# A change to weight loads, the transposes of h, row sums and unread products in a fused attention and expert kernel

## The chip, the cores and the metric

The kernel runs on one core of a Trainium2 chip. The metric is the device time of one execution in microseconds. The other cores of the chip do nothing for it. All inputs and outputs lie in the chip's main memory as 32-bit floats; inside the core the kernel works in 16-bit floats, and its loads convert on the way.

## What is computed

Sliding-window attention over 8 batches of 8 heads, 576 positions and 64 columns per head, followed by a soft mixture of experts over the 4608 rows of 512 columns that the attention gives. There are 8 experts with 4 slots each.

```python
def _attn_ref(q, k, v):                       # q, k, v: [8, 8, 576, 64]
    scores = 1.0 / np.sqrt(D) * np.matmul(q, k.transpose(0, 1, 3, 2))
    mask = (rel >= 0) & (rel < 64)            # rel = row minus column
    attn = softmax(np.where(mask, scores, -1e9))
    return np.matmul(attn, v)

def _moe_ref(x, phi, w1, w2):                 # x [4608, 512], phi [512, 32], w1 [8, 512, 1024], w2 [8, 1024, 512]
    logits = x @ phi
    d = softmax of logits over the rows (axis 0)
    slot_input = (d.T @ x).reshape(8, 4, 512)
    for e in range(8):
        slot_out[e] = np.maximum(slot_input[e] @ w1[e], 0.0) @ w2[e]
    c = softmax of logits over the 32 slots (axis 1)
    return c @ slot_out                       # [4608, 512]
```

q, k and v are 28.3 MB together, w1 and w2 16.8 MB each, and the output is 9.4 MB.

## The kernel before

**Two parts.** The first part goes through 16 units; a unit is half of the heads of one batch (`units`, line 58). Each unit has three steps j. In a step the tensor engine (PE) transposes v (`stage_t2`), multiplies k with q (`stage_s`), transposes pieces of the next batch's q, k and v (`stage_t1`) and multiplies the exponentials with v (`stage_av`). After both halves of a batch, `stage_xt`, `stage_logit`, `stage_ex` and `stage_slot` (taken from the list `todo`, one per step) transpose the batch's rows, form exp(logits) in `ET` and add to the slot inputs in `acc`. The last batch has its own version (`fin_...`, lines 547 to 567). From unit 2 on (`MAN = 14`, line 508) the order on PE, the scalar engine (ACT) and the vector engine (DVE) is the order of the program.

The second part starts when the slot inputs are complete. For each expert e: `expert_h(e)` multiplies the slot inputs with w1 (h is 4 slots by 1024, kept as four groups of 256 columns), `expert_t(e)` transposes h by products with `sel`, a view of the identity, and `expert_o(e, half)` multiplies with w2 into `sop[half]`. `row_sums(bp)` (line 621) adds up the columns of `ET` for a pair of batches, so that `crcp` holds the reciprocals for the second softmax; it is called for experts 0 to 3 (line 674). `stir(8)` (line 613) is eight products whose result nobody reads; it stands ahead of `expert_o(7, 0)`. Then `slots_out(half)` moves the result into `slot_oa`, and `combine` multiplies `ET` with it, scales by `crcp` and sends pieces of the output off through SP's queue. The first six pieces are done in column halves (`early`), the others whole (`late`).

**Loads.** Nearly all loads are issued by POOL in program order, on one queue: per batch q, k, v in rows of 4608 bytes (`load_batch`, line 67), and between them the weights in the order of `w_order` (line 481), a few per batch (`issue_loads`, line 485). A weight of one expert is 2 MB at its source. `load_w(e, n)` (line 83) loads w1 in two pieces (n = 0, 1) of 1 MB with 8-KB rows, and w2 in two pieces (n = 2, 3): for experts 0 to 5 with 4-KB rows, for the last two (`NLAST`) by columns with 1-KB rows. The order of the last loads is w1 of experts 6 and 7, then the first column half of w2 of both, then the second halves. `w2_of` says where the rows of a product with w2 lie. Since w2's rows are dealt to partitions in twos, `expert_t` takes every second column of h (`f::2`) in two products of 128 columns.

POOL's DMAs use eight semaphores in turn: a DMA waits until the one eight places before it has landed. Tiles come from pools that are used in turn too, so that a load also waits for the last reader of the tile it replaces: two buffers each for `qn`, `kn`, `vn`, and the two halves of w2 of experts 4 to 6 take such buffers (`w2h`).

Of the kernel before, what the change touches and what calls it, by code (L numbers as in the profile page):

```python
# [16 lines left out]
def kernel(  # L17
# [10 lines left out]
    nc = tc.nc  # L28
# [45 lines left out]
    w1_t, w2_t = {}, {}  # L74
    NLAST = 2

    def w2_of(e, f, cols):

        if e >= E - NLAST:
            return w2_t[e, cols.start // (D // 2)][:, f, :]  # L80
        return w2_t[e, f // 4][:, f % 4, cols]

    def load_w(e, n):
# [4 lines left out]
        if n == 2 and (e < E - 4 or e == E - 1):  # L88
            if e < E - 4:
                t = pw2.tile([128, NFC, D], FP16, name="w2s", tag="w2s")  # L90
            else:
                t = pxb.tile([128, NFC, D], FP16, name="w2l", tag="x_bp")
            for m in range(2):
# [6 lines left out]
        if n < 2:  # L100
            c = slice(2 * n, 2 * n + 2)
            nc.gpsimd.dma_start(out=w1_t[e][:, c], in_=moe_w1[e].rearrange("(p c) f -> p c f", p=128)[:, c])  # L102
        elif cols:
            c = slice(D // 2 * (n - 2), D // 2 * (n - 1))
            nc.gpsimd.dma_start(out=w2_t[e, n - 2], in_=moe_w2[e].rearrange("(c p) d -> p c d", p=128)[:, :, c])
        else:
            g = slice(2 * n - 4, 2 * n - 2)
            nc.gpsimd.dma_start(out=w2_t[e, n - 2].rearrange("p (g c) d -> p g (c d)", c=2),
                                in_=moe_w2[e].rearrange("(g p c) d -> p g (c d)", p=128, c=2)[:, g])
# [224 lines left out]
    def stage_xt(b, part):  # L334
# [11 lines left out]
        if part < 2:  # L346
            nc.vector.tensor_copy(out=moe[b][:, :, 2 * part:2 * part + 2, :],
                                  in_=tr[:, :, :].rearrange("p (k n) q -> p k n q", n=2))
# [129 lines left out]

    w_order = [(e, n) for e in range(E - NLAST) for n in range(4)]
    last = range(E - NLAST, E)
    w_order += [(e, n) for e in last for n in range(2)] + [(e, n) for n in range(2, 4) for e in last]

    def issue_loads(u):
        if u == 1 or u > 1 and u % 2 == 0:
            b = u // 2 + 2
            if b < B:
                load_batch(b)
                for _ in range(2 + b % 2):  # L490
                    load_w(*w_order.pop(0))
            else:

                for _ in range(len(w_order) if u > nu - 4 else 8):
                    load_w(*w_order.pop(0))

    load_batch(1)
    load_w(*w_order.pop(0))
    todo = []
# [10 lines left out]
    for u in range(nu):  # L510
# [7 lines left out]
        for j in range(3):  # L518
# [15 lines left out]
            if pend is not None:  # L534
# [5 lines left out]
                if pj == 2 and units[pu][1] == 1:  # L540
                    b = units[pu][0]
                    todo += [lambda b=b, p=p: stage_xt(b, p) for p in range(2 + b % 2)]
                    todo += [lambda b=b: stage_logit(b), lambda b=b: stage_ex(b), lambda b=b: stage_slot(b)]
            pend = (u, j)
# [43 lines left out]
    def expert_t(e):  # L588

        th = ps2.tile([128, 2, 4, SPE], FP32, name="th", tag="cp", bufs=4)  # L590
        for f in range(2):
            c = h_t[e][:, f::2] if e < E - NLAST else h_t[e][:, 128 * f:128 * f + 128]
            nc.tensor.matmul(th[:, f], c, sel[:, :, SPE * e:SPE * e + SPE], start=True, stop=True)
        hT = hTs[e % NLAST]
        if e >= NLAST:
            nc.vector.memset(hT[:, :, SPE * (e - NLAST):SPE * (e - NLAST) + SPE], 0.0)
        nc.vector.tensor_copy(
            out=hT[:, :, SPE * e:SPE * e + SPE].rearrange("p (g f) s -> p f g s", f=2), in_=th[:, :])
# [14 lines left out]
    def stir(n):  # L613

        if "stir" not in h_t:
            h_t["stir"] = ps2.tile([128, 256], FP32, name="stir", tag="hp")
        for _ in range(n):
            nc.tensor.matmul(h_t["stir"][:, :], ident[:, :], ET[:, 0, 0:256], start=True, stop=True)


    def row_sums(bp):
        rs = ps2.tile([128, T], FP32, name="rs", tag="cp", bufs=4)
        for j in range(T):
            nc.tensor.matmul(rs[:, j:j + 1], ET[:, bp, j::T], quarter[:, :], start=True, stop=True)
        nc.vector.reciprocal(crcp[:, bp, :], rs[:, :])
# [27 lines left out]
    with tc.manual_schedule(engines={mybir.EngineType.PE, mybir.EngineType.Activation, mybir.EngineType.DVE}):  # L653
# [10 lines left out]
        for e in range(E):  # L664
# [4 lines left out]
            if e > E - NLAST:  # L669
                stir(8)  # L670
# [3 lines left out]
            if e < B // 2:  # L674
                row_sums(e)
        slots_out(0)
        for n, p in enumerate(early):
            combine(*p, halves[0])
            if n >= len(early) - NLAST:
# [36 lines left out]
```

The softmax here doesn't subtract the row's maximum and nothing guards it: scores larger than these inputs give would overflow.

## Time and profile before

| What | us |
|---|---|
| median of 7 runs (179.59 to 180.77) | 180.36 |
| profiled execution, its own time | 180.72 |
| span of the profiled execution | 178.9 |
| PE busy | 138.2 (77%) |
| ACT busy | 121.5 (68%) |
| DVE busy | 117.8 (66%) |
| POOL busy | 40.1 (22%) |
| read from main memory | 61.93 MB |
| written to main memory | 9.44 MB |

The span is what the engines' instructions cover; some 1.8 us of the time lie around it. The DMA rate in the profile counts bytes at the destination: while loads convert 32 bits to 16, twice as many bytes leave the source. PE's clock is full until 148 us and half in some stretches after it. The attention part takes until about 133 us, the products of the experts until 150 us, and the output from 151 us to the end.

### The profile page before, as it was taken

How to read it: one execution, taken by the hardware profiler on the slowest of the kernel's cores; microseconds unless marked ns; L12 is line 12 of the kernel's file. 1: busy time of each engine (PE TensorE's matmuls, PEld its weight loads, DVE VectorE, ACT ScalarE, POOL GpSimd, SP SyncE). 2: the span in 40 equal slices, each digit the busy share in tenths (PEclk: the TensorE clock that was granted, in tenths of full speed). 3: DMA queues.
4: the chain of work that ended last, by engine and by line, in shares of the span. 5: the costliest groups of instructions: out<-in, count | busy, mean ns of one | idle time of the engine just before them, and what ended most of it. 6: DMA issues, size and time to landing. Idle time of an engine off the chain costs nothing.

```text
span 178.9 us, 6645 instructions
## 1 busy us (share of the span) xinstructions
PE 138.2 (77%) x2929; PEld 101.9 (57%) x2929; DVE 117.8 (66%) x283; ACT 121.5 (68%) x202; POOL 40.1 (22%) x65
## 2 busy tenths in 40 slices
PE   0659977997999997989989798888879976888200
PEld 0448766775777775767667576655556743444000
DVE  5634869769787888876876977597862212599300
ACT  2656696996998898789699598943644223699300
POOL 8601634212132133121232122222311000000000
PEclk9999999999999999999999999999999996699855
DMA  5999999999999999999999999999999999999994
GB/s 176 310 205 212 213 212 216 209 212 212 218 210 210 212 211 213 214 211 212 213 213 210 214 212 215 210 214 211 213 213 216 197 198 151 336 351 411 427 422 188
DMA packets 22812, 41.71 MB, mean 233 GB/s; under 512 B 1792, under 2 KB 10496, under 8 KB 22784
## 3 DMA queue, kind: packets, MB, share of 16 engines
q0 software_dynamic: 16784, 30.08, 90.7%
q1 hardware_dynamic: 6000, 11.21, 16.6%
q8 instruction: 23, 0.38, 0.8%
q14 instruction: 5, 0.04, 0.1%
HBM read 61.93 MB, written 9.44 MB: 399 GB/s over the span
## 4 chain that ended last, share of the span: by engine, by line
PE 38%; ACT 22%; DMA 16%; DVE 13%; issue 4%; SPq 1%; ACTq 0%
DMA w2l<-in_moe_w_dram 12%; PE tr L192 11%; ACT pm L281 6%; DVE vT L197 6%; ACT qT L199 6%; PE tr L236 5%; DMA first<-in_v_dram 4%; PE sc L264 4%; ACT ob L640 4%; PE cp L636 4%; PE av L307 3%; PE sc L271 3%; PE tr L345 3%; ACT kT L199 3%; DVE x_bp L315 3%
## 5 line engine op out<-in xcount | busy, mean ns | idle before, releaser
L281 ACT ACTIVATE pm<-sc 128x1024 f16<-128x1024 f32 (+1 forms) x46 | 38.1, 828 | 16.9 <-PE sc L271 16.9
L199 ACT COPY qT<-tr 128x640 f16<-128x640 f16 (+1 forms) x30 | 23.4, 865 | 1.4 <-PE tr L192 1.4
L199 ACT COPY kT<-tr 128x640 f16<-128x640 f16 (+1 forms) x30 | 23.7, 880 | 0.2 <-PE tr L192 0.2
L315 DVE TENSOR_TENSOR x_bp<-av,rc 128x512 f16<-128x512 f32 x32 | 22.1, 691 | 1.1
L307 PE MATMUL av<-vw,pm 128*64 128x65 f16 x576 | 19.3, 197 | 3.1 <-DVE x_bp L315 1.0
L197 DVE COPY vT<-tr 128x512 f16<-128x512 f16 (+1 forms) x17 | 13.9, 836 | 8.3 <-PE tr L192 8.3
L192 PE MATMUL tr<-ident,qn 128*64 128x128 f16 x288 | 13.6, 234 | 7.0 <-ACT qn L502 5.3
L271 PE MATMUL sc<-qT,kT 64*128 64x64 f16 x576 | 17.9, 193 | 1.2 <-DVE kT L197 0.9
L642 DVE TENSOR_SCALAR ob<-cp,crcp 128x256 f32<-128x256 f32 (+1 forms) x25 | 13.9, 588 | 7.5 <-PE cp L636 7.3
L271 PEld LDWEIGHTS <-kT 64*128 64x128 f16 x576 | 15.1, 97 | 5.7 <-ACT kT L199 1.1
L307 PEld LDWEIGHTS <-pm 128*64 128x64 f16 x576 | 15.7, 112 | 4.4 <-DVE x_bp L315 1.9
L264 PE MATMUL sc<-rep,hide 64*128 64x512 f16 (+1 forms) x96 | 17.1, 342 | 1.1 <-ACT pm L281 1.1
L640 ACT ACTIVATE ob<-cp,crcp 128x256 f32<-128x256 f32 (+1 forms) x26 | 13.9, 563 | 2.5 <-PE cp L636 1.8
L192 PEld LDWEIGHTS <-qn 128*64 128x64 f16 x288 | 10.1, 116 | 9.1 <-ACT qn L502 5.3
L192 PE MATMUL tr<-ident,vn 128*64 128x128 f16 x288 | 12.9, 232 | 2.9 <-ACT kT L199 1.1
L236 PE MATMUL tr<-ident,vT 128*128 128x128 f16 x128 | 10.5, 224 | 5.9 <-DVE rc L313 3.6
L199 ACT COPY vT<-tr 128x640 f16<-128x640 f16 x15 | 14.0, 933 | 1.4 <-PE tr L192 1.3
L636 PE MATMUL cp<-slot_oa,ET 128*128 128x256 f16 (+1 forms) x51 | 12.8, 351 | 2.7 <-ACT slot_oa L611 0.9
L102 POOL DMA_DIRECT2D w1s<-in_moe_w_dram x16 | 8.9, 554 | 21.1 <-DMA w1s<-in_moe_w_dram 7.3
L237 DVE COPY vw<-tr 128x1024 f16<-128x1024 f16 x16 | 11.0, 689 | 3.7 <-PE tr L236 3.7
L236 PEld LDWEIGHTS <-vT 128*128 128x128 f16 x128 | 8.1, 100 | 9.2 <-ACT vT L199 6.5
L192 PE MATMUL tr<-ident,kn 128*64 128x128 f16 x288 | 12.3, 233 | 0.1
(115 smaller groups left out, 228.7 us busy)
## 6 DMA issues: line engine op xcount, KB each, us to landing
w1s<-in_moe_w_dram POOLq DMA_DIRECT2D x16, 512.0 KB, 20.6
out_dram<-ob SPq DMA_DIRECT2D x6, 768.0 KB, 7.7
w2s<-in_moe_w_dram POOLq DMA_DIRECT2D x8, 512.0 KB, 20.4
qn<-in_q_dram POOLq DMA_DIRECT2D x7, 576.0 KB, 20.5
kn<-in_k_dram POOLq DMA_DIRECT2D x7, 576.0 KB, 20.8
vn<-in_v_dram POOLq DMA_DIRECT2D x7, 576.0 KB, 19.1
w2h<-in_moe_w_dram POOLq DMA_DIRECT2D x6, 512.0 KB, 20.2
out_dram<-ob SPq DMA_DIRECT2D x8, 384.0 KB, 4.3
```

The source lines that it names most:

```text
L192: nc.tensor.transpose(tr[64 * x:64 * x + 64, j, :], src[:, x, 64 * (t0 + j):64 * (t0 + j) + 64], ident[:, :])
L197: nc.vector.tensor_copy(out=o, in_=i)
L199: nc.scalar.copy(out=o, in_=i)
L236: nc.tensor.transpose(tr[:, 2 * w + h, :], vT[:, h, 64 + 128 * w:192 + 128 * w], ident[:, :])
L264: nc.tensor.matmul(sc[x][:, 0:128 * n], hide[64 * x:64 * x + 64, :], rep[64 * x:64 * x + 64, 0:2 * n, :], start=True, stop=False, skip_gro ...
L271: nc.tensor.matmul(sc[x][:, o:o + 64], st["kT"][64 * x:64 * x + 64, h, 64 * i:64 * i + 128], st["qT"][64 * x:64 * x + 64, h, 64 * i:64 * i ...
L281: nc.scalar.activation(pm[:, :, 0:2 * n, :], sct[:, :, 0:128 * n].rearrange("p x (w q) -> p x w q", q=64), AF.Exp, scale=scale)
L307: nc.tensor.matmul(av[r0:r0 + 64, kk, 65 * (w // 2):65 * (w // 2) + 65], pm[:, x, h * n + w, :], st["vw"][:, i, 2 * h + x, 0:65], start=Tr ...
L315: nc.vector.tensor_tensor(out=xb[:, c0:c0 + 2, 256 * half:256 * half + 256].rearrange("p c (k d) -> p k c d", d=64), in0=avv[:, :, :, 0:64 ...
L636: nc.tensor.matmul(cp[:, :], ET[:, bp, j::T], slot_oa[:, cols], start=True, stop=True)
L640: nc.scalar.activation(ob[:, g, :], cp[:, :], AF.Copy, scale=cr)
L642: nc.vector.tensor_scalar(out=ob[:, g, :], in0=cp[:, :], scalar1=cr, scalar2=None, op0=ALU.mult)
```

## The change

**w1** is loaded in one DMA of 2 MB with 16-KB rows, instead of two with 8-KB rows.

**w2 of experts 0 to 5** is dealt to partitions in fours, so that rows are 8 KB, in two DMAs of 1 MB. For expert 2 (`ES`) the load is cut another way: three lots of 4 partitions and a fourth one, each preceded by a small load of 2 or 12 partitions from phi (`pass_over`, into a tile nobody reads), and then the other 112 partitions in one DMA. That is nine DMAs of POOL's queue in place of two.

**Order of the loads.** The first weight load is now the first half of w2 of expert 0, then its w1. A w1 counts as two in the number of weight loads per batch, and the debt is carried over (`want`). The nine DMAs of expert 2 count as one.

**expert_t** for experts 0 to 5 makes h's transpose in eight products of 64 columns instead of two of 128. Those of experts 6 and 7 are as before.

**Row sums** of pairs 0, 1 and 2 are made in the three steps of unit 14, that of pair 3 ahead of `expert_o(6, 0)`. **Unread products**: one in each step of units 14 and 15 (five in all), and nine instead of eight ahead of `expert_o(7, 0)`.

**stage_xt** of batch 6 copies with ACT instead of DVE. **In the early pieces**, `expert_o(6, 1)`, `expert_o(7, 1)` and `slots_out(1)` come one piece earlier.

```diff
+    def w2_strips(e, p0, p1):
+        nc.gpsimd.dma_start(
+            out=w2_t[e][p0:p1].rearrange("p (g c) d -> p g (c d)", c=4),
+            in_=moe_w2[e].rearrange("(g p c) d -> p g (c d)", p=128, c=4)[p0:p1])
+    turns = []
+    def pass_over(n):
+        if not turns:
+            turns.append(const.tile([12, 4, 2, 16], FP16, name="turn"))
+        t = turns[0][0:n, len(turns) - 1]
+        turns.append(n)
+        nc.gpsimd.dma_start(out=t, in_=moe_phi[0:2 * n, 0:16].rearrange("(p c) s -> p c s", c=2))
...
-        if n < 2:
-            c = slice(2 * n, 2 * n + 2)
-            nc.gpsimd.dma_start(out=w1_t[e][:, c], in_=moe_w1[e].rearrange("(p c) f -> p c f", p=128)[:, c])
+        if n == 0:
+            nc.gpsimd.dma_start(out=w1_t[e].rearrange("p c f -> p (c f)"),
+                                in_=moe_w1[e].rearrange("(p c) f -> p (c f)", p=128))
...
-            g = slice(2 * n - 4, 2 * n - 2)
-            nc.gpsimd.dma_start(out=w2_t[e, n - 2].rearrange("p (g c) d -> p g (c d)", c=2),
-                                in_=moe_w2[e].rearrange("(g p c) d -> p g (c d)", p=128, c=2)[:, g])
+        elif e == ES:
+            if n == 2:
+                for i in range(4):
+                    pass_over(12 if i else 2)
+                    w2_strips(e, 4 * i, 4 * i + 4)
+                w2_strips(e, 16, 128)
+        else:
+            nc.gpsimd.dma_start(out=w2_t[e, n - 2].rearrange("p c d -> p (c d)"),
+                                in_=moe_w2[e].rearrange("(g p c) d -> g p (c d)", p=128, c=4)[n - 2])
...
+            o, i = moe[b][:, :, 2 * part:2 * part + 2, :], tr[:, :, :].rearrange("p (k n) q -> p k n q", n=2)
+            if b == B - 2:
+                nc.scalar.copy(out=o, in_=i)
+            else:
+                nc.vector.tensor_copy(out=o, in_=i)
...
-    w_order = [(e, n) for e in range(E - NLAST) for n in range(4)]
+    w_order = [(e, n) for e in range(E - NLAST) for n in (0, 2, 3)]
-    w_order += [(e, n) for e in last for n in range(2)] + [(e, n) for n in range(2, 4) for e in last]
+    w_order += [(e, 0) for e in last] + [(e, n) for n in range(2, 4) for e in last]
...
-                for _ in range(2 + b % 2):
-                    load_w(*w_order.pop(0))
+                want[0] += 2 + b % 2
+                while want[0] > 0:
+                    e, n = w_order.pop(0)
+                    load_w(e, n)
+                    want[0] -= 1 if n else 2
...
-                for _ in range(len(w_order) if u > nu - 4 else 8):
+                for _ in range(len(w_order) if u > nu - 4 else 5):
                     load_w(*w_order.pop(0))
...
+    w_order[0:2] = [(0, 2), (0, 0)]
     load_w(*w_order.pop(0))
+    want = [0]
...
+            if u == nu - 2:
+                row_sums(j, ps, "tr")
+            if u >= nu - 2:
+                stir(1, ps, "tr", 4)
...
-        for f in range(2):
-            c = h_t[e][:, f::2] if e < E - NLAST else h_t[e][:, 128 * f:128 * f + 128]
-            nc.tensor.matmul(th[:, f], c, sel[:, :, SPE * e:SPE * e + SPE], start=True, stop=True)
+        th = ps2.tile([128, 4, 2, SPE], FP32, name="th", tag="cp", bufs=4)
+        for c in range(4):
+            for x in range(2):
+                nc.tensor.matmul(th[64 * x:64 * x + 64, c], h_t[e][:, c::4], sel[:, x::2, slots], start=True, stop=True)
+        nc.vector.tensor_copy(out=o.rearrange("p (g c) s -> p c g s", c=4), in_=th[:, :])
...
-            if e > E - NLAST:
-                stir(8)
+            if e == E - 2:
+                row_sums(B // 2 - 1, ps2, "cp")
+            if e == E - 1:
+                stir(9, ps2, "hp", 2)
             expert_o(e, 0)
...
-            if e < B // 2:
-                row_sums(e)
...
-            if n >= len(early) - NLAST:
-                expert_o(last[n - len(early)], 1)
-        slots_out(1)
+            if n >= len(early) - 1 - NLAST and n < len(early) - 1:
+                expert_o(last[n - len(early) + 1], 1)
+            if n == len(early) - 2:
+                slots_out(1)
```

POOL's DMAs of the changed kernel in their order, around expert 2: q, k, v of batch 5; w1 of expert 2 (2 MB); 2-partition load, 4-partition strip, 12-partition load, strip, 12, strip, 12, strip; the 112-partition piece; q, k, v of batch 6; w1 of expert 3; q, k, v of batch 7.

## The prediction

> **What bounds the kernel now.** I read the rate rows of the page first, then the table by stage, then POOL's own timeline, then PE's timeline at the end and around batch 6.
>
> ```profile
> DMA  5999999999999999999999999999999999999994
> GB/s 176 310 205 212 213 212 216 209 212 212 218 210 210 212 211 213 214 211 212 213 213 210 214 212 215 210 214 211 213 213 216 197 198 151 336 351 411 427 422 188
> ...
> 20.00:30.00 10.00, 7.77 (x204) 6.48 (x206) 8.29 (x18) 7.75 (x10) 4.53 (x7) 1.00 1.09 211
> ...
> 145.00:148.00 3.00, 1.75 (x34) 1.14 (x25) 0.34 (x3) 0.30 (x1) 0.00 (x0) 1.00 1.46 198
> 150.00:155.00 5.00, 4.46 (x31) 2.26 (x28) 2.91 (x7) 3.47 (x8) 0.00 (x0) 0.50 0.92 223
> ```
>
> The DMA engines are busy from the first load to the last store. Loads run at about 212 GB/s at the destination, so 424 at the source, at every time up to 139 us; the 1-KB rows of the last four loads bring it to 198. So the DMA stream is the bound, although PE has the longest busy row. How a load comes to be issued, POOL's timeline shows (start, duration, what; in brackets the idle time before it and what ended it):
>
> ```profile
> 25.58 0.72 POOL L70 DMA_DIRECT2D kn<-in_k_dram  x1 [2.42 <-PE av L307]
> 28.58 0.72 POOL L70 DMA_DIRECT2D vn<-in_v_dram  x1 [2.28 <-PE av L307]
> 29.29 0.72 POOL L108 DMA_DIRECT2D w2s<-in_moe_w_dram  x1
> 30.00 0.56 POOL L102 DMA_DIRECT2D w1s<-in_moe_w_dram  x1
> 32.53 0.54 POOL L102 DMA_DIRECT2D w1s<-in_moe_w_dram  x1 [1.97 <-DMA vn<-in_v_dram]
> 35.23 0.71 POOL L70 DMA_DIRECT2D qn<-in_q_dram  x1 [2.16 <-PE tr L192]
> 38.84 0.72 POOL L70 DMA_DIRECT2D kn<-in_k_dram  x1 [2.90 <-PE tr L247]
> 42.31 0.72 POOL L70 DMA_DIRECT2D vn<-in_v_dram  x1 [2.75 <-PE tr L192]
> 44.12 0.72 POOL L108 DMA_DIRECT2D w2s<-in_moe_w_dram  x1 [1.09 <-DMA kn<-in_k_dram]
> ```
>
> The load at 44.12 waited for kn to land, and that kn is the one issued at 25.58, eight rows above it. A load is issued when the one eight places before it has landed. Today eight outstanding loads are up to 8 MB or 20 us of work, so the queue never runs dry. At the end, PE waits for these loads:
>
> ```profile
> 145.35 0.21 PE L593 MATMUL th<-ident,h_sb 128*128 128x16 f16 x2
> 146.81 0.40 PE L606 MATMUL sop<-w2h,hT 128*32 128x256 f16 x8 [1.25 <-DMA w2h<-in_moe_w_dram]
> 147.14 1.05 PE L618 MATMUL stir<-ET,ident 128*128 128x256 f16 x8
> 149.46 0.62 PE L606 MATMUL sop<-w2l,hT 128*32 128x256 f16 x8 [1.27 <-DMA w2l<-in_moe_w_dram]
> ```
>
> And at batch 6 there is little reserve:
>
> ```profile
> 87.80 0.69 PE L192 MATMUL tr<-ident,qn 128*64 128x128 f16 x18
> ```
>
> The trace keeps sixteen landing times for each DMA, one per DMA engine. Batch 6's q is complete at 87.10, and the transposes that read it start at 87.80: 0.7 us. The same records show that the engines are uneven. A load lands on its fastest engine 1.45 us before the slowest at 10 us, 2.5 us at 40 us, 3.5 us at 90 us, and 4.63 us at the last load (150.04 to 154.67). There one engine is at 154.67, five at 153.5, two at 152.1 to 152.3, eight between 150.0 and 151.2. The packets of the instruction queue (23 of 16 KB, some 0.95 us each, repeating with a period of eight) fit that: eight engines carry them, eight don't. The slowest engine has no gap from 10 us to the end: its outputs follow its last load directly, and its end (177.96, the fastest 176.77) is the end of the output. So what counts is that one engine's total work and any hole in it.
>
> **What the Trainium skill says.** "DMA: Bandwidth & Descriptors", section "Specifications", gives a first-byte latency of about 1 us for DMAs issued by POOL and 0.6 us for those of SP. The trace agrees for SP: the first output is issued at 151.46 for 0.36 us and its first packet starts at 152.32, 0.5 us after the issue ends. For POOL no place shows it, as its queue is never empty; q of batch 0 has its issue ended at 2.69 and its first packet at 6.37, with SP's loads before it on the same engines, so 3.7 us is an upper bound. The same page, section "Why a DMA increments its semaphore by 16 and not by 1", says that a DMA with few partitions uses k consecutive engines from a round-robin cursor. No load of the kernel before has so few partitions; I take it only for the purpose of the strips: always the same four engines. "Runtime: NRT & Kernel Launch", section "Instruction fetch mechanics", says that PE's instruction memory is refilled in 16-KiB blocks, 128 KiB in all; the period of eight agrees. "TensorE: Matmul & The Clock Gate", Part 1, puts PE at half clock after a mostly idle window of about 3.4 us. The trace shows half clock from 148.60 to 155.43, after PE had worked 1.45 of 3.1 us.
>
> **The change part by part**, against the span of 178.9.
>
> *Longer rows.* Spacing of landings on one engine that carries little else: 1 MB of w1 (8 packets of 8 KB at the source per engine) 2.45 us, 1 MB of w2 (16 packets of 4 KB) 2.50 us. So a packet costs about 5.5 ns beyond its bytes. q with 16 packets of 4608 bytes takes 2.79, as the same rule gives. w1 whole has 8 packets fewer per expert: 8 x 8 x 5.5 ns = 0.35 us. w2 in 8-KB rows has 16 fewer for each of six experts: 6 x 16 x 5.5 = 0.53 us. Sum -0.88 us. If a 16-KB row is cut in two anyway, -0.53.
>
> *The strips.* Four engines get four more rows, and all get 7 instead of 8 of the 112: a row of 16 KB is 0.61 us (2 x 0.306). The slowest engine loses 0.61 us if it isn't one of the four; those four get +1.8 us, which an engine without instruction fetches can carry, as it is 3.4 to 4.6 us ahead. -0.61 us.
>
> *The strips in POOL's queue.* Nine DMAs stand where two stood, and the rule of eight still holds. Counted in the order of its program, the fourth strip waits for the w1 of expert 2, which is eight places before it; the 112-partition piece comes after it. So when the 112 partitions are issued, all that was ahead of them on the queue has landed, except loads of a few rows. The queue runs dry. For the slowest engine the hole is: from its last byte to the semaphore 0.3 us (last packets start about 0.3 us before the landing), to POOL's next issue 0.3 (32.25 landed, 32.53 issued), the issue of the strip about 0.45 (half of the 0.7 to 0.9 of larger ones), that of the 112 partitions 0.7, and 1.0 for the first byte by the skill. That is 2.75 us. Low end 2.1 (latency as SP's, a strip's issue of 0.3); high end 5.4 (latency 3.7). I take 2.75. A hole below zero isn't possible. After it there is nothing with which the slowest engine could catch up.
>
> Sum for the slowest engine: 2.75 - 0.61 - 0.88 = +1.3 us.
>
> *Batch 6's q.* It now comes after four weight units instead of three in batch 5's turn, and after the hole. w1 of expert 2 ends where the second w1 of that turn ended, 80.67, less 0.3 for the rows so far, and the semaphore's 0.3: 80.05. Plus the hole 2.75, seven rows 4.3, q 2.79, semaphore 0.3: 90.2, and 91.1 on the engine that has an instruction fetch there (83.19). PE wants it at 87.80. PE waits 3.3 us, everything on ACT and DVE with it. A wait of that length may cost PE the full clock for 6.8 us (as at 148.6), 0 to 2.5 us more; I take 1.3.
>
> *Row sums, unread products, copies.* Three row sums (0.70 us each) and five products (0.13 each, from 1.05 for eight) enter units 14 and 15, 2.75 us of PE. There PE is idle 15 to 25% (3.37, 3.02, 3.33 of 4 us), and DVE loses two copies of 0.68 to ACT (1.2 to 3.0 busy of 4). Between -0.5 and +1.5; I take +0.5. In the expert part four row sums go (spacing of experts 1.88 with, 1.14 without: -0.74 each, -2.96), and six more transposes for each of six experts come, at 0.04 to 0.06 us each: +1.5. So -1.4 us up to expert 5.
>
> PE at expert 6 then: 145.35 + 3.3 + 1.3 + 0.5 - 1.4 = 149.1. A row sum 0.74, `expert_o(6, 0)` 0.35, nine products 1.2 follow: 151.4. The weights it waits for land at 149.42 + 1.3 = 150.7. So PE would be some 0.7 us late, and the first output comes 1.9 us later than before (151.4 for 149.46). The fastest engine ends 1.9 later, 178.7; the slowest at 177.96 + 1.3 = 179.3. With the parts uncertain by more than this difference, and most errors pointing up (a later q, a lower clock), I add 0.4: the span grows by 1.7, to 180.6. The same 1.7 on the median gives 182.1; the profiled execution, 0.36 above the median, would be at 182.4.
>
> *The early pieces.* `slots_out(1)` one piece earlier waits for the load that lands at 154.67 before, and holds one piece back by some 0.5 us, which outputs queued on SP (issued 2.5 us ahead) cover. Nothing. If the queue were empty, 0.5 us.
>
> **The rivals.**
> 1. *The hole is as computed, and PE takes over.* The wait for q, the low clock and the added PE work all come at their upper ends: 4 + 2.5 + 1.5 - 1.4 = 6.6 us on the chain to expert 6. PE reaches 152.0 there, and the first output comes 4.8 us late (152.0 + 2.3 = 154.3, for 149.46). The fastest engine then ends at 181.6, 3.6 after the old end: 184.0. For it: 0.7 us of reserve at batch 6. Against it: attention isn't held by PE alone.
> 2. *The queue does not run dry for the slowest engine, and the kernel gets faster.* It decides from a hole under 1.5 us on: if the strips land on that engine they fill 1.8 us of it, or if the issues overlap with the tail of w1. With no loss: -0.88 - 0.61 = -1.5, 178.9. For it: the sums of the rows are well measured, and a hole is seen nowhere in the trace. Against it: the wait stands in the program, and four times an issue has followed a landing by 0.3 us.
> 3. *The gains and the hole cancel* (hole of 1.5 to 2): 180.4. For it: only the upper bound of POOL's latency is measured.
>
> **How the numbers follow.** Forecast 0.52 (range 180.9 to 183.6), rival 1 0.20, rival 2 0.17, rival 3 0.11. About 0.3%, 0.54 us, is what the runs can tell from no change. Faster by more than that: rival 2, 0.17. Within: rival 3 with small parts of its neighbours, 0.11. Slower: forecast and rival 1, 0.72. The range leaves out half of rival 2 and half of rival 1's upper side: 179.0 to 185.0.
>
> **What would show it.** A slice of the rate row near 81 us clearly below 212, and two issues on POOL right after w1 of expert 2 has landed: the hole. PE idle on the transposes of q of batch 6 until about 91 us: the wait. Spacing on one engine of 2.43 us per MB of w1 and 2.45 of w2: the packets. `sop` of w2l at 151 us or later: the end. If there is no dip near 81 us, the prediction is wrong, and the time falls towards 179.

## The result and the profile after

The changed kernel takes 184.41 us (median of 12 runs, 183.41 to 187.11), against 180.36 of the kernel before (31 runs, 179.47 to 181.12). The ratio is 1.0227, with a 95% interval of 1.0204 to 1.025; it leaves out two of the twelve runs, 186.46 and 187.11 us, which fell in a slower state. The profiled execution took 184.09 us with a span of 182.0; that of the kernel before took 180.72 with 178.9. So the two profiles differ by 3.4 us and the medians by 4.05.

The direction is as forecast. The size is not: 4.05 us for 1.7, and 184.41 lies outside the range of 180.9 to 183.6.

The rate rows of the changed kernel's page show one place where the stream of loads breaks:

```profile
DMA  5999999999999999939999999999999999799996
GB/s 185 301 205 211 213 213 223 208 208 214 227 201 211 217 209 214 226 71 143 205 212 225 203 212 216 221 210 221 209 220 218 199 196 195 219 385 400 429 423 253
```

One slice is 4.55 us. The dip is in the 18th and 19th slice, 77 to 86 us; everywhere else from the third slice to the output the row stands between 195 and 227, where before it was 197 to 218 (and 151 in the last slice ahead of the output). POOL's timeline of the changed kernel says what was issued there (start, duration, what; in brackets the idle time before and what ended it):

```profile
57.40 0.57 POOL L119 DMA_DIRECT2D w1s<-in_moe_w_dram  x1
...
67.66 0.57 POOL L87 DMA_DIRECT2D w2s<-in_moe_w_dram  x1 [1.90 <-DMA w2s<-in_moe_w_dram]
70.39 0.56 POOL L98 DMA_DIRECT2D turn<-in_moe_phi_dram  x1 [2.16 <-DMA qn<-in_q_dram]
73.25 0.59 POOL L87 DMA_DIRECT2D w2s<-in_moe_w_dram  x1 [2.30 <-DMA kn<-in_k_dram]
76.01 0.56 POOL L98 DMA_DIRECT2D turn<-in_moe_phi_dram  x1 [2.17 <-DMA vn<-in_v_dram]
80.84 1.25 POOL L87 DMA_DIRECT2D w2s<-in_moe_w_dram  x2 [4.27 <-DMA w1s<-in_moe_w_dram]
82.16 0.72 POOL L70 DMA_DIRECT2D qn<-in_q_dram  x1
```

The issue at 80.84 waited for the w1 that was issued at 57.40, eight places above it. By then everything else on the queue was 4-partition strips and loads of a few rows. The stage table of the changed kernel (stretch in us; then length, busy time and count of PE, PEld, DVE, ACT and POOL; granted PE clock, DMA share, GB/s) shows how empty the queue was, and what PE did in the next 12 us:

```profile
79.00:80.00 1.00, 0.00 (x0) 0.00 (x0) 0.67 (x2) 0.99 (x2) 0.00 (x0) 1.00 0.42 74
80.00:81.00 1.00, 0.98 (x25) 0.71 (x25) 0.45 (x1) 0.00 (x0) 0.16 (x1) 1.00 0.09 5
81.00:82.00 1.00, 1.00 (x30) 0.84 (x25) 0.95 (x3) 0.83 (x1) 1.00 (x2) 1.00 0.06 16
82.00:83.00 1.00, 1.00 (x8) 0.54 (x7) 0.83 (x3) 1.00 (x3) 0.93 (x3) 1.00 0.89 86
83.00:84.00 1.00, 0.94 (x27) 0.72 (x28) 0.29 (x1) 1.00 (x5) 1.00 (x2) 1.00 0.73 74
84.00:88.00 4.00, 3.63 (x95) 2.72 (x93) 3.38 (x7) 3.25 (x8) 2.98 (x5) 1.00 1.02 200
88.00:92.00 4.00, 0.48 (x18) 0.27 (x14) 1.84 (x4) 1.02 (x1) 0.68 (x1) 1.00 1.09 208
92.00:96.00 4.00, 3.79 (x64) 2.99 (x66) 1.58 (x4) 2.26 (x3) 1.08 (x2) 0.60 1.11 213
148.00:151.00 3.00, 3.00 (x64) 1.96 (x54) 0.34 (x3) 0.47 (x1) 0.00 (x0) 0.53 1.45 197
```

In the five microseconds from 79 to 84, 74 + 5 + 16 + 86 + 74 = 255 KB land where 212 GB/s would give 1060. That is 3.8 us of the average engine. The rate from 82 to 84 is as telling as the near zero before it: POOL has issued the large piece by 82.1 and q and k by 83.6, and yet the engines move less than half. The DMA share in these two rows, 0.89 and 0.73, says that they weren't idle: their packets took longer. In the trace's packet records, the packets of 4096 bytes (at the destination) that start between 82.75 and 84 took 0.72 us in the median, and 0.324 from 60 to 76 us. From 88 to 92 PE has 0.48 us of work in 4 us. PE's timeline of the changed kernel names the wait, and shows the end of the expert part:

```profile
88.08 0.40 PE L294 MATMUL sc<-qT,kT 64*128 64x64 f16 x16
92.21 0.69 PE L215 MATMUL tr<-ident,qn 128*64 128x128 f16 x18 [3.73 <-DMA qn<-in_q_dram]
97.38 0.69 PE L215 MATMUL tr<-ident,kn 128*64 128x128 f16 x18
...
145.62 0.41 PE L652 MATMUL th<-ident,h_sb 128*64 128x8 f16 x8
147.31 0.97 PE L661 MATMUL sop<-w2s,hT 128*32 128x256 f16 x16 [1.28 <-issue]
...
152.46 0.40 PE L661 MATMUL sop<-w2h,hT 128*32 128x256 f16 x8
152.80 1.16 PE L515 MATMUL stir<-ET,ident 128*128 128x256 f16 x9
153.88 0.40 PE L661 MATMUL sop<-w2l,hT 128*32 128x256 f16 x8
```

Before, these transposes of batch 6's q began at 87.80 and the product with w2l at 149.46, and the latter waited 1.27 us for its load. Now that product waits for nothing: PE comes 2.3 us later than the load, which lands at 151.60. The chain that ended last, in order of time (start, duration, what), runs over the w1 that held the queue, then over the q that stood behind it, then over PE:

```profile
57.40 23.15 DMA w1s<-in_moe_w_dram
81.40 0.69 POOL w2s L87
82.16 10.01 DMA qn<-in_q_dram
92.21 0.69 PE tr L215 x18
```

The landing records of the DMAs give the rest, on the slowest DMA engine: the last load lands at 157.21 (154.67 before), the last output at 181.00 (177.96). On the fastest engine the last output lands at 180.57 (176.77).

Two readings are open. Either the broken stream costs these microseconds through the loads, or PE's wait for q, with the low clock after it, pushes the first output back, as rival 1 had it.

### The profile page after: what moved, and what is told of

Its sections match the earlier page's. It is cut to its first block, busy times and chain, and to the rows that moved or that the text cites. A ratio compares the mean times of both kernels' runs of the same rounds, so it can differ in the third digit from the quotient of the medians.

```text
span 182.0 us, 6729 instructions
## 1 busy us (share of the span) xinstructions
PE 139.7 (77%) x2971; PEld 104.5 (57%) x2971; DVE 116.3 (64%) x281; ACT 123.4 (68%) x204; POOL 37.9 (21%) x64
## 4 chain that ended last, share of the span: by engine, by line
PE 35%; DMA 23%; ACT 19%; DVE 11%; issue 4%; POOL 1%; SPq 0%; ACTq 0%; DVEq 0%; POOLq 0%
DMA w1s<-in_moe_w_dram 13%; PE tr L215 7%; ACT pm L304 6%; DMA qn<-in_q_dram 5%; DMA first<-in_v_dram 4%; ACT ob L682 4%; ACT qT L222 4%; DVE vT L220 4%; ACT kT L222 3%; PE sop L661 3%; PE tr L259 3%; PE sc L287 3%; PE cp L678 3%; PE tr L368 3%; PE av L330 3%
## 5 line engine op out<-in xcount | busy, mean ns | idle before, releaser
L287 PE MATMUL sc<-rep,hide 64*128 64x512 f16 (+1 forms) x96 | 17.6, 345 | 1.4 <-ACT pm L304 1.0
L678 PE MATMUL cp<-slot_oa,ET 128*128 128x256 f16 (+1 forms) x51 | 11.8, 316 | 2.5 <-ACT ob L682 0.9
L336 DVE RECIPROCAL rc<-av 128x8 f32<-128x8 f32 x32 | 6.4, 199 | 10.0 <-PE av L330 9.4
```

The costliest lines, as they stand in the source:

```text
L287: nc.tensor.matmul(sc[x][:, 0:128 * n], hide[64 * x:64 * x + 64, :], rep[64 * x:64 * x + 64, 0:2 * n, :], start=True, stop=False, skip_gro ...
L678: nc.tensor.matmul(cp[:, :], ET[:, bp, j::T], slot_oa[:, cols], start=True, stop=True)
```

## The experiments

All kernels compute the whole result. Each ratio is against the kernel before on the same chip, whose median was 180.06, 180.23 or 180.36; so the ratios can be compared between lines, and the medians only within some 0.3 us. The last load comes from one profiled execution each.

| Experiment | median us | ratio, 95% interval | last load, slowest engine |
|---|---|---|---|
| changed kernel | 184.41 | 1.0227 [1.0204, 1.025] | 157.21 |
| no strips | 179.97 | 0.9981 [0.9963, 1.0] | 153.78 |
| strips for expert 3 | 182.61 | 1.0134 [1.0098, 1.017] | 156.46 |
| loads of before, rest changed | 180.29 | 1.0005 [0.9988, 1.0022] | 154.25 |
| longer rows alone | 180.11 | 1.0002 [0.9985, 1.0019] | 153.76 |
| rows of w1 alone | 180.40 | 1.0006 [0.9987, 1.0024] | 154.11 |
| rows of w2 alone | 179.94 | 0.9985 [0.9971, 0.9999] | 153.32 |
| a w1 between the strips | 180.83 | 1.0034 [1.0017, 1.0052] | 153.48 |
| expert 3, a w1 between | 180.83 | 1.002 [1.0005, 1.0036] | 154.63 |
| few-row loads, spread | 180.12 | 0.9999 [0.9982, 1.0017] | 153.96 |
| few-row loads, in a row | 184.06 | 1.0209 [1.0178, 1.0239] | 157.48 |
| products in PE's wait | 183.77 | 1.0194 [1.0164, 1.0225] | 157.43 |
| rows of w2, rest changed | 180.18 | 0.9999 [0.9976, 1.0022] | 153.29 |

### Without the strips, and with the strips elsewhere

The first takes the strips out; w2 of expert 2 is then loaded like that of the other experts. The second makes them for expert 3, whose w2 stands behind q, k and v of batch 7. There no load of attention follows the hole.

```diff
-    ES = 2
+    ES = -1
```

> The changed kernel with w2 of expert 2 loaded like the others, in two DMAs, and all else as changed. Theory (the nine DMAs run POOL's queue dry, q of batch 6 comes late and PE is late from then on): no dip of the rate near 80 us, PE's wait for q of batch 6 (3.7 us) gone, last-but-two load (first half of w2 of expert 7) at about 148.6 us on the slowest engine, time 179.3 to 179.8. Rival (the row sums, unread products and eight-part transposes make PE late by themselves): the time stays above 182.

```diff
-    ES = 2
+    ES = 3
```

> The nine DMAs are given to expert 3, so that they stand behind q, k and v of batch 7 and no load of attention comes after the hole. Theory with two costs (the hole in the DMA stream, and apart from it the wait of PE for q): the rate dips near 108 us by as much as it did near 80, PE has no wait for q, and the product that starts the output waits for its load at about 151.6 us instead of being 2.3 us later than it; time 182.2 to 182.8. Rival (the hole alone makes the time, the wait of PE is covered): 184.4 as the changed kernel.

The rate row of the kernel without strips, by its page:

```profile
GB/s 170 309 202 213 214 210 221 216 204 214 220 207 214 215 211 210 226 205 210 214 224 204 211 217 214 217 218 215 210 224 208 198 195 132 203 384 406 421 426 276
```

and that of the kernel with the strips at expert 3:

```profile
GB/s 172 314 206 212 213 212 223 211 205 215 227 202 210 217 209 212 228 202 212 214 224 201 214 98 134 220 209 227 205 221 216 204 195 197 320 366 410 419 430 212
```

Without strips the dip is gone, and so is the loss: 179.97 us. So the whole loss of the change hangs on the strips. With the strips moved, the dip moves with them, to the 24th and 25th slice (104 to 113 us), and costs 182.61 - 179.97 = 2.64 us. There PE's timeline has the product with w2l at 151.12, held by its load, which lands at 151.08:

```profile
151.12 0.40 PE L661 MATMUL sop<-w2l,hT 128*32 128x256 f16 x8 [0.31 <-DMA w2l<-in_moe_w_dram]
```

So a hole costs 2.6 us where the first output waits for its load and not for PE. The last load is 2.68 us later than without strips, as much as the time. In the changed kernel the last load is 157.21 - 153.78 = 3.43 us later than without strips, 0.75 more than here. Why the earlier hole is the dearer one no run settles.

The kernel without strips shows a second thing. Its profiled execution took 181.18 us, 1.2 above the median, and PE was late in it although no load was: the slot inputs' product begins at 137.71 (133.44 before, 138.88 in the changed kernel), and the product with w2l comes 2.2 us after its load, which lands at 148.50:

```profile
150.66 0.40 PE L661 MATMUL sop<-w2l,hT 128*32 128x256 f16 x8
```

The delay begins with a pause of 1.57 us at 49.2, for which no wait is shown, and half clock from 51.2 to 54.6. So a PE that is four microseconds late at the slot inputs is no sign of a hole, and not all of the changed kernel's 5.44 us there need come from q.

### The order alone

These are the same nine DMAs of expert 2 and the same w1, but the w1 is issued after the second strip instead of ahead of the first. So a DMA of 2 MB stands in the middle of the small ones (`HELD` is 2).

```diff
         if n == 0:
-            nc.gpsimd.dma_start(out=w1_t[e].rearrange("p c f -> p (c f)"),
-                                in_=moe_w1[e].rearrange("(p c) f -> p (c f)", p=128))
+            if e == HELD:
+                held.append(e)
+            else:
+                load_w1(e)
...
                 for i in range(4):
+                    if i == 2:
+                        load_w1(held.pop())
                     pass_over(12 if i else 2)
```

> The changed kernel with w1 of expert 2 (2 MB) issued after the second strip instead of ahead of the first. The same DMAs, bytes and rows stand ahead of q of batch 6; but the piece of 112 partitions now waits for the first strip, and w1 is still running then. Theory (the rule of eight makes the hole): no dip near 80 us, PE's wait for q of batch 6 falls from 3.7 us to 1 to 2.5 (one weight more ahead of it, no hole), time 179.5 to 181. Rival (DMAs of a few rows are slow by themselves, 0.16 us on every engine and more): the dip stays and the time stays above 183.

POOL's timeline of that kernel, at the place where the changed one stood still:

```profile
67.19 0.57 POOL L104 DMA_DIRECT2D w1s<-in_moe_w_dram  x1 [1.85 <-DMA w2s<-in_moe_w_dram]
...
76.65 0.56 POOL L98 DMA_DIRECT2D turn<-in_moe_phi_dram  x1 [3.13 <-DMA vn<-in_v_dram]
77.20 1.25 POOL L87 DMA_DIRECT2D w2s<-in_moe_w_dram  x2
78.51 0.72 POOL L70 DMA_DIRECT2D qn<-in_q_dram  x1
```

and its rate row:

```profile
GB/s 183 309 205 212 212 212 224 205 210 216 219 207 213 216 211 209 223 159 208 212 224 207 210 217 217 218 208 222 211 220 216 196 195 176 302 384 410 429 422 183
```

The large piece is issued at 77.8 instead of 81.4, while the w1 is still on its way, and the dip shrinks from 71 and 143 to one slice of 159. The transposes of batch 6's q begin at 90.03 without a wait for q. That is 2.2 us later than in the kernel before, since PE itself gets there late, as without strips (90.05); q is complete at 88.60. The time is 180.83, at a ratio of 1.0034 for 1.0227: about 3.5 us less than the changed kernel, with the same bytes, rows, strips and DMAs. So it is the order of the DMAs in the queue, not the strips as such.

The same for the strips of expert 3, with the next large load (w1 of expert 4) in their middle (two more lines, not shown, keep the count of the loads):

```diff
                 for i in range(4):
+                    if i == 2:
+                        load_w(*w_order.pop(0))
                     pass_over(12 if i else 2)
```

> The strips given to expert 3, behind batch 7's q, k and v, and w1 of expert 4 issued after the second strip. Against the run with the strips late: only the hole goes. Theory: no dip near 108 us, time down by the hole, to 179.0 to 180.0; rival (few-row DMAs slow by themselves): 182.6 as before.

The time is 180.83, a ratio of 1.002 for 1.0134 of the strips in a row. The dip is down to one slice of 182 GB/s, not gone, and the 179.0 to 180.0 that were expected are missed. The last load is at 154.63, 0.85 later than without strips at all; in the run before it was at 153.48, 0.30 earlier. Whether the strips save the 0.61 us of the slowest engine, these two don't tell, as a small dip is left in both.

### A dry queue in the kernel before

The cleanest form of the question: the kernel before, all of its loads untouched, plus eight loads of 12 partitions from phi into a tile that nobody reads. In the first version one follows each of eight weight loads of experts 4 and 5; in the second the eight stand in a row ahead of those.

```diff
-                for _ in range(len(w_order) if u > nu - 4 else 8):
+                few = u <= nu - 4
...
+                for _ in range(8 if few else len(w_order)):
                     load_w(*w_order.pop(0))
+                    if few and not False:
+                        pass_over(12)
```

> The kernel before with eight loads of 12 rows from phi added (128 bytes each row, into a tile nobody reads), one after each of the eight weight loads of experts 4 and 5, behind batch 7's q, k and v. The large loads in between keep the queue full. If a load of a few rows costs 0.16 us on every engine (the spacing of their landings in the changed kernel): loads end 1.3 us later, time 181.3 to 181.8. If they cost only their packets: 180.2 to 180.5.

```diff
+                few = u <= nu - 4
+                for _ in range(8 if few and True else 0):
+                    pass_over(12)
+                for _ in range(8 if few else len(w_order)):
                     load_w(*w_order.pop(0))
```

> The same eight loads one after another, ahead of the first of those weight loads. The eighth waits for the last large load to land, so the queue runs dry once. Theory: the hole is 2.5 us from the last landing to the first packet and about 1 us of slow start after it, most of the eight loads' own time falls into it; loads end 3 to 3.7 us later than before, time 183 to 184. Rival (no hole): the time of the run with the loads spread.

The second version's POOL timeline:

```profile
110.24 0.55 POOL L90 DMA_DIRECT2D turn<-in_moe_phi_dram  x1 [1.92 <-DMA w2s<-in_moe_w_dram]
112.69 0.55 POOL L90 DMA_DIRECT2D turn<-in_moe_phi_dram  x1 [1.90 <-DMA w2s<-in_moe_w_dram]
113.24 1.12 POOL L111 DMA_DIRECT2D w1s<-in_moe_w_dram  x2
```

and its stage table:

```profile
112.00:113.00 1.00, 0.94 (x25) 0.66 (x22) 0.29 (x1) 1.00 (x3) 0.31 (x1) 1.00 0.05 1
113.00:114.00 1.00, 1.00 (x47) 0.91 (x40) 0.17 (x1) 1.00 (x5) 1.00 (x3) 1.00 0.01 0
114.00:118.00 4.00, 3.64 (x87) 2.60 (x84) 3.93 (x8) 2.67 (x6) 4.00 (x7) 1.00 0.89 137
```

Spread, the eight loads cost nothing (0.9999). In a row they cost 3.7 us over the kernel before: almost nothing moves from 112 to 114, and 137 GB/s for four microseconds after that. The packets are slow here too: 0.91 us in the median from 114 to 115, 0.34 from 115 to 116. PE keeps its work through the hole (0.94 and 1.00 of 1), it has its slot inputs at 132.99 (133.44 before), and the product with w2l begins at 152.25, right after its load has landed at 152.21. So here the loss comes through the loads alone. The last load is at 157.48, 2.8 us later than before and a little less late than the 3 to 3.7 expected. That the time, 184.06, is so near the changed kernel's 184.41 is in part chance, as this kernel has its hole elsewhere and no longer rows. What it shows is that a dry queue can cost 3.7 us without PE being late for any other reason. The spread version also disposes of a third idea, that each load of a few partitions costs the engines a fixed time of its own.

### What PE's wait adds

In the changed kernel, 32 products whose result nobody reads fill the wait for batch 6's q, so that PE's clock isn't halved after it.

```diff
+                if u == 10 and j == 0:
+                    stir(32, ps, "tr", 4)
                 stage_t1(b, 3 * (u % 2) + j)
```

> The changed kernel with 32 unread products of 128x256 (some 3.7 us) ahead of the transposes of batch 6's q, where PE waits 3.7 us. If the half clock after that wait costs what the transposes of q and k show (4.41 us late at q, 4.85 at k): PE's clock is full there, attention is 0.4 us earlier, and the time falls by 0 to 0.5, to 184. If the low clock is the larger part of PE's delay: a fall of 1.5 or more, below 183.

PE's timeline of that kernel (cut at 96 us):

```profile
87.02 3.67 PE L515 MATMUL stir<-ET,ident 128*128 128x256 f16 x32
91.94 0.69 PE L215 MATMUL tr<-ident,qn 128*64 128x128 f16 x18 [1.25 <-DMA qn<-in_q_dram]
...
95.67 0.47 PE L215 MATMUL tr<-ident,kn 128*64 128x128 f16 x10
```

and its stage table:

```profile
88.00:92.00 4.00, 2.75 (x27) 2.21 (x27) 0.48 (x2) 0.21 (x1) 0.57 (x1) 1.00 1.09 207
92.00:96.00 4.00, 4.00 (x108) 3.40 (x109) 2.46 (x7) 3.55 (x5) 1.08 (x2) 1.00 1.12 216
```

The clock stays full (1.00 for 0.60 from 92 to 96). q itself arrives nearly as late as in the changed kernel (91.90 for 92.17), since nothing on the queue has changed. The transposes of k begin 1.71 us earlier, at 95.67 instead of 97.38, though those of q began only 0.27 earlier: so the low clock cost about 1.4 us there. The slot inputs' product comes at 136.74 instead of 138.88, and the product with w2l at 151.96 instead of 153.88: PE is 1.9 us earlier at the end and 0.1 behind its load (151.82). But the last load is at 157.43, as in the changed kernel, and the time falls by only 0.6 us, to 183.77, with overlapping intervals. Neither expectation had this: PE gains far more than 0.4 us, and the time doesn't follow. So when 1.9 us of PE's delay go, about 0.6 of the 4.05 us goes with them, and the rest stays.

### The other parts by themselves

The loads of the kernel before, with all the rest of the change (row sums, unread products, copies, early pieces), as an edit to the changed kernel:

```diff
-        if n == 0:
-            nc.gpsimd.dma_start(out=w1_t[e].rearrange("p c f -> p (c f)"),
-                                in_=moe_w1[e].rearrange("(p c) f -> p (c f)", p=128))
+        if n < 2:
+            c = slice(2 * n, 2 * n + 2)
+            nc.gpsimd.dma_start(out=w1_t[e][:, c], in_=moe_w1[e].rearrange("(p c) f -> p c f", p=128)[:, c])
...
-    w_order = [(e, n) for e in range(E - NLAST) for n in (0, 2, 3)]
+    w_order = [(e, n) for e in range(E - NLAST) for n in range(4)]
```

> The kernel before with the other half of the change alone: row sums and unread products in units 14 and 15, one row sum ahead of expert 6, ACT copies in batch 6, the early pieces one earlier; loads and transposes of h as before. Theory (DMA is the bound, PE has more than 1 us to spare at expert 6): within 0.4 us of before, 180.0 to 180.7. Rival (added PE work in units 14 and 15 reaches the end): 181 or more.

180.29, the time of before. The slot inputs' product begins at 133.41 (133.44 before). While the loads keep up, three row sums and five products more in attention cost nothing that the runs can tell.

The longer rows of both weights and the new order of the loads, without strips and without that rest, from the kernel before (wherever w2's rows are longer, h is transposed in eight products, as these rows need):

```diff
-        if n < 2:
-            c = slice(2 * n, 2 * n + 2)
-            nc.gpsimd.dma_start(out=w1_t[e][:, c], in_=moe_w1[e].rearrange("(p c) f -> p c f", p=128)[:, c])
+        if n == 0:
+            nc.gpsimd.dma_start(out=w1_t[e].rearrange("p c f -> p (c f)"),
+                                in_=moe_w1[e].rearrange("(p c) f -> p (c f)", p=128))
...
-            g = slice(2 * n - 4, 2 * n - 2)
-            nc.gpsimd.dma_start(out=w2_t[e, n - 2].rearrange("p (g c) d -> p g (c d)", c=2),
-                                in_=moe_w2[e].rearrange("(g p c) d -> p g (c d)", p=128, c=2)[:, g])
+            nc.gpsimd.dma_start(out=w2_t[e, n - 2].rearrange("p c d -> p (c d)"),
+                                in_=moe_w2[e].rearrange("(g p c) d -> g p (c d)", p=128, c=4)[n - 2])
...
-    w_order = [(e, n) for e in range(E - NLAST) for n in range(4)]
+    w_order = [(e, n) for e in range(E - NLAST) for n in (0, 2, 3)]
```

> The kernel before with longer rows alone: w1 whole in 16-KB rows, w2 of experts 0 to 5 in 8-KB rows, h transposed in eight parts, no strips; row sums, unread products, copies and early pieces as before. Theory (5.5 ns per packet saved): loads end 0.9 us earlier, time 179.3 to 179.8. Rival 1 (q of batch 7, which now has one weight more ahead of it, comes late): a wait of PE for it and 180.5 or more. Rival 2 (six more transposes per expert make PE late at expert 6): 180.3 to 181.

The kernel before with the longer rows of w1 and the new order alone:

```diff
-        if n < 2:
-            c = slice(2 * n, 2 * n + 2)
-            nc.gpsimd.dma_start(out=w1_t[e][:, c], in_=moe_w1[e].rearrange("(p c) f -> p c f", p=128)[:, c])
+        if n == 0:
+            nc.gpsimd.dma_start(out=w1_t[e].rearrange("p c f -> p (c f)"),
+                                in_=moe_w1[e].rearrange("(p c) f -> p (c f)", p=128))
```

> The kernel before with w1 whole in 16-KB rows and the order of loads that goes with it, alone. If rows of 16 KB make PE's instruction fetches later (the pauses of PE named issue were 1.6 us in sum before and 2.8 with both kinds of longer rows): these pauses stay at 2.5 or more, and the time is 180.0 to 180.6 although loads end 0.35 earlier. If not: 179.7 to 180.1.

The kernel before with the longer rows of w2 alone:

```diff
-            g = slice(2 * n - 4, 2 * n - 2)
-            nc.gpsimd.dma_start(out=w2_t[e, n - 2].rearrange("p (g c) d -> p g (c d)", c=2),
-                                in_=moe_w2[e].rearrange("(g p c) d -> p g (c d)", p=128, c=2)[:, g])
+            nc.gpsimd.dma_start(out=w2_t[e, n - 2].rearrange("p c d -> p (c d)"),
+                                in_=moe_w2[e].rearrange("(g p c) d -> g p (c d)", p=128, c=4)[n - 2])
```

> The kernel before with w2 of experts 0 to 5 in 8-KB rows and h transposed in eight parts, alone; w1 and the order as before. No packet is longer than before. Loads end 0.5 us earlier. If the fetch pauses come from the 16-KB rows: they stay at 1.6 us in sum and the time is 179.5 to 180.0. If the six more transposes per expert reach the end: 180.4 or more.

Last, w2's rows together with the row sums, products, copies and early pieces of the change, by an edit to the changed kernel:

```diff
-        if n == 0:
-            nc.gpsimd.dma_start(out=w1_t[e].rearrange("p c f -> p (c f)"),
-                                in_=moe_w1[e].rearrange("(p c) f -> p (c f)", p=128))
+        if n < 2:
+            c = slice(2 * n, 2 * n + 2)
+            nc.gpsimd.dma_start(out=w1_t[e][:, c], in_=moe_w1[e].rearrange("(p c) f -> p c f", p=128)[:, c])
...
-        elif e == ES:
-            if n == 2:
-                for i in range(4):
-                    pass_over(12 if i else 2)
-                    w2_strips(e, 4 * i, 4 * i + 4)
-                w2_strips(e, 16, 128)
```

> The kernel before with w2 of experts 0 to 5 in 8-KB rows, h in eight parts, and the second half of the change (row sums and unread products in units 14 and 15, ACT copies, early pieces); w1 and the order of loads as before, no strips. Theory (DMA is the bound, 0.5 us are saved, PE has the reserve): 179.5 to 180.0, faster than both kernels. Rival (PE's pauses eat it): 180.2.

The last load comes at 153.76, 154.11, 153.32 and 153.29, for 154.67 before. Yet three of the four times can't be told from that of before, and the rows of w2 alone are at 0.9985 [0.9971, 0.9999], only just below it. Two expectations of a faster kernel are missed: 180.11 for 179.3 to 179.8 with both rows, 180.18 for 179.5 to 180.0 with w2's rows and the rest.

The last of the four has early loads and a late PE: its product with w2l begins at 149.87, when its load had landed at 148.00. PE stood idle 0.89 us at 48.6, 1.03 at 55.5, 1.21 at 79.4 and 1.10 at 109.8, with nothing shown that it waited for. Such pauses are in every trace here, shorter in the kernel before (0.75 at 78.4, 0.83 at 108.5). They don't hang on the rows of 16 KB: those of over half a microsecond before 150 us add up to 1.6 us in the kernel before, to 3.3 with w1's rows, but also to 2.8 with w2's and to 2.6 with the eight loads spread, which leaves all weights as they were. All 40 pauses of 0.7 us or more between 20 and 150 us, in the fourteen traces, begin close to the end of a 16-KB packet of the instruction queue, from 0.1 us before it to 0.9 after, though these packets come some 6 us apart. That points to waits for instructions; no run takes the packets away.

## Why the prediction was half right

**What bounds the kernel** was read rightly. The stream of loads sets the time, and its damage is the result: the last load moved by 2.54 us in the profile, and without the strips the loss is gone (179.97).

**The place and the cause of the hole** were right: the queue of eight in order, the w1 of expert 2, slices near 81 us, both issues directly after its landing. The order alone moved 3.5 us.

**The size of the hole is the step that failed.** The prediction says "I take 2.75. A hole below zero isn't possible". Between the slowest landings of the w1 (80.55) and of the large piece (89.04) the trace has 8.49 us, of which the seven rows are 4.3: a hole of 4.2 us. The terms ahead of the first byte hold: from the landing of w1 to the first packet of the large piece (82.79) it is 2.2 us, and with the 0.3 of the semaphore 2.5. "DMA: Bandwidth & Descriptors", section "Specifications", puts POOL's first byte at about 1 us; here it came 0.7 us after the issue had ended (82.09), so this term was rather too large. What was missing is what comes after the first byte. I took the stream to be back at 212 GB/s at once. It moved 86 and 74 from 82 to 84, and the large piece landed 5.2 us after its first packet on the fastest engine and 6.25 on the slowest. Less the 4.3 of its rows and 0.3 for the semaphore, the slow start is 0.6 to 1.7 us. The eight small loads in the kernel before show the same, 137 GB/s for 4 us after 2 us of next to nothing. Why the first packets take longer stays open.

The strips, with the hole, were to cost 2.75 - 0.61 = 2.14 us; the last load has 3.43. A hole of 4.2 less 0.61 is 3.6, so the credit of 0.61 fits, but no run shows it by itself.

**Longer rows**: predicted -0.88 us; the last load of the two kernels with both rows and no strips is 0.89 and 0.91 earlier than before. This hit is weaker than it looks. Two kernels with the old rows have their last load at 154.25 and 153.96, so that one profile is uncertain by 0.7, and w2's rows alone come out earlier than both together. The spacing of the landings, which the forecast named as the sign, is steadier. On the fastest engine, in the median, 2 MB of w1 take 4.87 us in one DMA and 4.91 in two, and 1 MB of w2 2.46 for 2.48 (longer rows alone, and the kernel before). Over all these loads that is some 0.6 us; the 2.50 from which the forecast worked was a high reading for w2. In the time, the rows of both weights bring nothing (1.0002).

**Batch 6's q**: predicted on the engines at 90.2 to 91.1, PE's wait 3.3; measured 90.75 to 92.17 and 3.73. Right, and late by the same slow start. The low clock after it was there for one window, 92.8 to 96.2. Against the kernel before, the transposes of k are only 0.44 us later than those of q (4.85 for 4.41). But with the clock full this lateness falls from 4.14 to 3.14, so the clock cost 1.4 us, near the 1.3 that were taken. "TensorE: Matmul & The Clock Gate", Part 1, gives the clock a window of about 3.4 us, and the 3.4 us from 92.8 to 96.2 agree.

**Row sums, products, copies**: predicted +0.5 with -0.5 as the low end; measured 0 where the loads are on time. In the changed kernel PE's delay grows from 4.06 us at the last batch's v to 5.44 at the slot inputs. How much of that is this work wasn't separated; the pauses of PE, which made it 4.3 us late without strips, have their part in it.

**The expert part**: predicted -1.4 us up to expert 5, with nothing changed between it and the transposes of expert 7. From the slot inputs to these it is 148.57 - 137.71 = 10.86 us without strips, for 11.91 before: -1.05. In the changed kernel it is 12.91, +1.0, since a pause of 1.28 us at 146.0 and half clock from 147.4 to 150.9 came in between. So PE reached the product with w2l at 153.88, where the forecast had 151.4 and rival 1 had 154.3.

**Rival 1** gave 184.0, and so the time, but by luck: its mechanism is not what costs most of it. Its late PE is there, and what it is worth was measured: about 0.6 us when 1.9 of PE's delay are taken away. The reckoning of the profile agrees. Before, the last output came 177.96 - 154.67 = 23.29 us after the last load on the slowest engine. The same after 157.21 is 180.50; measured is 181.00. That leaves 0.5 for PE's lateness at the first output, and the remaining 2.5 of the 3.04 us came with the loads. Rivals 2 and 3 are out: the queue does run dry, on the slowest engine too, and by more than the gains.

The sum in the profile: rows -0.9 and strips with hole +3.4 at the last load, and 0.5 for PE, 3.0 us. The first two rest on the single profile without strips, so each may be off by some tenths. The medians differ by 1 us more than this. 0.7 of it is that the profiled execution of before lies 0.36 above its median and that of the changed kernel 0.32 below; 0.3 lies outside the span.

## What to carry to other kernels

A look-ahead that is counted in DMAs, as in this kernel, is worth only the bytes of these DMAs. Small loads in a row use it up, and then the queue waits for the last large one to land and starts again from nothing. So put a large load between small ones: the same eight loads cost 0 or 3.7 us by their order. When the price of an empty queue is worked out, the slow microseconds after its first byte belong to it, and a gain that one single profile shows at the last load needs runs before it is believed.

## What was not expected of the hardware

- A DMA stream that has run dry is not back at its rate with the first packet: 86 and 74 GB/s in the two microseconds in which it restarts, and 137 over four in the other case, where 212 is usual. The engines are not idle then. Their first packets take two to three times as long: 0.72 us in the median (82.75 to 84 us in the changed kernel), 0.91 (114 to 115 with the eight loads in a row) and 0.94 (109 to 110 with the strips of expert 3), for 0.324.
- Loads of 12 partitions in a full queue are free: eight of them, 0.9999 [0.9982, 1.0017].
- PE's clock is at half from 147.44 to 150.85, 3.4 us, after a pause of only 1.28 us (146.03 to 147.31) in the changed kernel. A pause of 1.49 us at 78.0, in the kernel with a w1 between the strips of expert 3, left it full. So the length of a pause doesn't decide it alone.
- Every longer pause of PE without a shown cause begins within 0.9 us of the end of a packet of its instruction queue (40 of 40).
